# Half-tile input loads, a paced fold and single steps in the first block of an FFT-plus-ReGLU kernel

## The chip, the cores and the metric

The kernel runs on one core of a Trainium2 chip. The metric is the device time of one execution in microseconds (us). Engine names follow the profile: PE is the matmul engine, PEld its weight load, DVE the vector engine, ACT the scalar engine, POOL the GpSimd engine, SP the engine whose queue issues most DMAs.

Before the change the median was 692.59 us of three runs (692.4 to 693.47).

## The reference

```python
X = np.fft.fft(np.fft.fft(x, axis=1), axis=2).real     # x: 8 x 3008 x 256, float32
h = X.reshape(24064, 256)
out = (np.maximum(h @ w_gate, 0) * (h @ w_val)) @ w_out # 256 -> 1536 -> 256
```

The kernel never forms X in full. It uses the symmetry of the transform of a real signal: row s and row 3008 - s share most of their work. The second transform is folded into the weights at the start.

## The kernel before

Each of the 8 batches is three blocks of 12 steps, so there are 288 steps in 24 blocks. A step is one slice of 128 hidden columns: gate matmuls (`G`), value matmuls (`V`), and products of both, `h`. Two steps form a pair. A pair's direct products are made by DVE, its mirrored products by POOL (from batch 0's second block on). The output matmuls of a block run during the block after it.

While the steps of batch b run, the input of a later batch is prepared in three stages:

- The load: x of batch b+2 comes into `xl` (17 of 32 rows of each partition) and, in mirrored partition order by an indirect DMA on POOL, into `xh` (the other rows).
- The fold, on POOL: sums and differences of mirrored rows and columns, in pieces, into `eo`. It overwrites `xl` and reads `xh`; there is one buffer of each.
- Stage 1 for batch b+1: matmuls on `eo`, a copy to DRAM and back in another layout (the shuffle, `Td`), a small matmul (`rotate`), then stage 2, whose results `pq` and `nb` feed the steps.

```python
def load_x(b, q):
    xl = xp.tile([96, J, D], F32, tag="xl", name="xl")           # J = 17, D = 256
    xh = xp.tile([96, NB // 2, D], F32, tag="xh", name="xh")     # NB = 32
    for p0, n in ((0, 80), (80, 14)):
        q.dma_start(out=xl[p0:p0 + n], in_=...)
    nc.gpsimd.indirect_dma_start(out=xh[...], in_=..., in_offset=...ix[:, b:b + 1]...)
    xt[b] = (xl, xh, tp.tile([NA, J, D], BF16, tag="eo", name="eo"))

def fold(b, eng):                       # a generator: one piece at each yield
    for lo in range(1, J - 1, xc):      # xc is 3 for batches 1 and 2, then 2
        eng.tensor_tensor(...)                                    # L98
        yield eng.tensor_tensor(x1[:, :, 1:D], x1[:, :, 1:D], ...)  # L100
        for op, o in ((ALU.add, 1), (ALU.subtract, H + 1)):
            yield eng.tensor_tensor(e1[...], x1[:, :, 1:H], ...)  # L103
    # ... (the two end rows)

# first number: step of the load; second: step at which the fold begins; then stage 1,
# shuffle, rotate, stage 2 (all counted from the first step of the batch)
plan = {0: (18, 24, (18, 19, 20, 21, 22, 23, 24, 25), 26, 32, (33, 34, 35, 37, 39, 41)),
        1: (7, 13, (7, 8, 10, 11, 13, 14, 16, 17), 18, 25, (26, 28, 29, 31, 34, 35)),
        2: (7, 13, (4, 5, 7, 10, 11, 13, 16, 17), 18, 25, (26, 28, 29, 31, 34, 35))}

def between(t):                         # once a step
    for fn in extra.get(t, ()): fn()
    while folds and next(folds[0], folds) is folds:   # one fold piece a step
        folds.pop(0)

for p in range(n + NF // 2):            # the main loop, by pairs
    t = 2 * p
    ...
    # block 0 (split(t) is False): V gets direct and mirror parts one after the other, on DVE
    value(t, 0); value(t, 1); value(t + 1, 0); value(t + 1, 1)
    ...; direct_h(p)                    # both steps' direct products
    ...; value(t, 2); value(t + 1, 2)   # mirror parts, into the same accumulators
    # next iteration: mirror_value(p - 1), both steps' mirrored products
```

In block 0 POOL is still folding batch 1's x, so both products are made by DVE there, and the mirror part of `V` may only be added once DVE has used the direct part.

## Time and profile before

| what | value |
|---|---|
| median time | 692.59 us |
| profiled span | 691.2 us |
| a block without fold (batches 6 and 7) | 24.6 to 25.0 us |
| block 0 | 34.9 us |
| block 2 | 31.1 us |
| middle block of batches 2 to 5 | 27.8 to 29.4 us |

Block times are taken from the first gate activation of one block to that of the next. From the profile page of the kernel before: the span, the busy time of each engine with its share of the span, and the rows of PE, POOL and the granted clock (the share of its full clock that PE was given) over 40 equal slices in tenths (9 is 90% or more). The last line follows the chain of work that ended last back from the end, as shares of the span by engine.

```profile
span 691.2 us, 11747 instructions
...
PE 636.6 (92%) x4200; PEld 414.0 (60%) x4231; DVE 548.6 (79%) x630; ACT 432.7 (63%) x846; POOL 512.6 (74%) x412
...
PE   7776897998999989998999989998999999999995
...
POOL 9539458995999589975999579974999555555552
PEclk8799998999999999999999999999999999999998
...
PE 46%; POOL 24%; DMA 13%; DVE 7%; issue 5%; ACT 2%; SPq 1%; POOLq 0%; DVEq 0%; ACTq 0%
...
```

PE is near 9 in most slices and has dents at 7 and 8. From the 10th slice on, each dent stands beside or just behind a low POOL digit, after which POOL goes to 9: POOL waits and then has more than it can do at once. POOL and DMA make up 37% of the chain. The next excerpt, the list of waits, says for what (who waited for whom: us in total, times, longest).

```profile
...
POOL h L538 <- DVE E L546: 99.5, 57, 7.5
...
DVE E L525 <- POOL h L538: 42.3, 32, 4.1
...
POOL eo L98 <- DMA xl<-in_x_dram: 26.4, 4, 7.0
POOL eo L98 <- DMA xh<-in_x_dram,ix: 23.4, 3, 10.5
...
```

The first line costs nothing by itself: POOL is simply ahead. The last two lines are fold pieces that wait for their x to land, 49.8 us in seven waits. They matter because POOL works in order and mirrored products are queued behind the fold piece. The second line is DVE waiting for those products.

Busy time by stretch, for block 0, block 2, the middle and last block of batch 2, and a block without fold. The columns are the stretch and its length, then busy us (and instructions) of PE, PEld, DVE, ACT, POOL, the granted PE clock, the DMA share and GB/s.

```profile
...
38.51:73.41 34.90, 24.30 (x123) 9.66 (x123) 17.32 (x19) 15.64 (x30) 23.52 (x26) 0.95 0.49 94
99.32:130.40 31.08, 27.37 (x178) 17.46 (x176) 21.63 (x25) 17.68 (x35) 24.97 (x20) 0.89 0.42 118
236.68:264.96 28.28, 24.86 (x165) 16.43 (x166) 21.98 (x25) 16.68 (x34) 21.29 (x18) 1.00 0.51 131
264.96:290.35 25.39, 25.17 (x185) 16.79 (x183) 21.46 (x25) 18.21 (x37) 24.92 (x23) 1.00 0.20 52
550.48:575.52 25.04, 24.70 (x165) 16.42 (x166) 21.91 (x25) 16.79 (x35) 13.99 (x7) 1.00 0.39 104
...
```

In the last line PE is busy 24.70 of 25.04 us: this is the bound by PE. In the third, PE needs nearly the same, 24.86 us, but the block takes 28.28.

One of these waits on POOL's timeline (start, duration, what, and in brackets the idle time before it and what ended it), inside that block:

```profile
...
225.85 0.96 POOL L85 DMA_INDIRECT xh<-in_x_dram,ix  x1
...
235.78 2.30 POOL L538 TENSOR_TENSOR h<-gm,E 128x992 bf16<-128x992 f32 x1 [1.96 <-DVE E L546]
244.75 0.22 POOL L98 TENSOR_TENSOR eo<-xl,xh 94x4 bf16<-94x4 f32 x1 [6.68 <-DMA xl<-in_x_dram]
...
246.27 2.27 POOL L538 TENSOR_TENSOR h<-gm,E 128x992 bf16<-128x992 f32 x1
...
```

DVE in the same stretch:

```profile
...
243.83 1.22 DVE L531 TENSOR_TENSOR h<-gs,V 128x1024 bf16<-128x1024 f32 x1
248.57 1.41 DVE L525 SCALAR_TENSOR_TENSOR E<-nb,af,V 128x512 f32<-128x512 bf16 x2 [3.52 <-POOL h L538]
...
```

The indirect part of the load is issued at 225.85; the direct part, which the piece waits for here, follows on SP behind output stores at 227.0. The first fold piece can start only at 244.75, 6.68 us after POOL became free, and the mirrored product after it starts at 246.27. DVE stood idle for 3.52 us before 248.57, and the block is 3.2 us longer than one without a fold.

### The profile page before, as it was taken

Reading aid. Unit: us, or ns where it says so; the run is one execution under the profiler, and the core shown is the slowest. Engines: PE = TensorE matmul, PEld = TensorE weight load, DVE = VectorE, ACT = ScalarE, POOL = GpSimd, SP = SyncE. Lnnn points to the kernel's source line nnn. Section 1 sums busy time; section 2 is a strip of 40 time slices with the busy share of each in tenths; the row PEclk is TensorE's granted clock in tenths of the full one; section 3 lists DMA queues with packets and bytes.
Section 4 is the critical chain, followed back from the end, with each engine's and each line's share of the span. In section 5 each row is a group of like instructions: output and inputs, shape, how many; then the busy total and the mean of one; then the engine's idle time right before and its main releaser. Section 6 shows DMA issues by size and latency. Waiting matters only on the chain.

```text
span 691.2 us, 11747 instructions
## 1 busy us (share of the span) xinstructions
PE 636.6 (92%) x4200; PEld 414.0 (60%) x4231; DVE 548.6 (79%) x630; ACT 432.7 (63%) x846; POOL 512.6 (74%) x412
## 2 busy tenths in 40 slices
PE   7776897998999989998999989998999999999995
PEld 3322564665666656665666656666566666666664
DVE  9725885777888878887888878886888888888981
ACT  5444583766677756676676756766576766756660
POOL 9539458995999589975999579974999555555552
PEclk8799998999999999999999999999999999999998
DMA  9691095155511932246521942246421223312113
GB/s 247 211 219 20 15 208 160 48 132 122 151 47 39 219 102 77 76 114 141 147 51 39 210 109 80 61 116 154 122 70 46 55 81 79 82 30 49 41 32 90
DMA packets 33982, 70.71 MB, mean 102 GB/s; under 512 B 5802, under 2 KB 23186, under 8 KB 31922
## 3 DMA queue, kind: packets, MB, share of 16 engines
q1 hardware_dynamic: 31284, 57.92, 33.0%
q0 software_dynamic: 2336, 11.80, 8.0%
q8 instruction: 33, 0.54, 0.3%
q10 hardware_dynamic: 304, 0.25, 0.1%
q14 instruction: 25, 0.20, 0.1%
HBM read 39.77 MB, written 30.96 MB: 102 GB/s over the span
## 4 chain that ended last, share of the span: by engine, by line
PE 46%; POOL 24%; DMA 13%; DVE 7%; issue 5%; ACT 2%; SPq 1%; POOLq 0%; DVEq 0%; ACTq 0%
PE po L570 19%; PE V L518 12%; POOL h L538 10%; DMA xl<-in_x_dram 7%; POOL xl L100 5%; DMA xh<-in_x_dram,ix 5%; POOL eo L103 5%; DVE E L525 4%; PE G L504 4%; PE G L510 4%; PE G L503 4%; POOL eo L131 2%; PE psw L274 1%; DVE h L531 1%; SPq L621 1%
## 5 line engine op out<-in xcount | busy, mean ns | idle before, releaser
L538 POOL TENSOR_TENSOR h<-gm,E 128x992 bf16<-128x992 f32 (+1 forms) x138 | 319.6, 2316 | 99.5 <-DVE E L546 99.5
L570 PE MATMUL po<-wo,h 128*128 128x256 bf16 (+2 forms) x2304 | 343.5, 273 | 0.6
L570 PEld LDWEIGHTS <-h 128*128 128x128 bf16 (+2 forms) x2304 | 233.9, 103 | 122.0 <-issue 1.8
L525 DVE SCALAR_TENSOR_TENSOR E<-nb,af,V 128x496 f32<-128x496 bf16 (+1 forms) x276 | 191.0, 734 | 101.6 <-PE V L518 47.7
L512 ACT ACTIVATE gm<-G 128x496 f32<-128x496 f32 (+1 forms) x288 | 170.3, 591 | 154.3 <-PE G L510 131.3
L531 DVE TENSOR_TENSOR h<-gs,V 128x992 bf16<-128x992 f32 (+2 forms) x144 | 172.0, 1194 | 6.1 <-ACT gs L505 5.1
L505 ACT ACTIVATE gs<-G 128x497 f32<-128x497 f32 (+2 forms) x288 | 169.4, 588 | 1.4 <-PE G L504 1.4
L546 DVE SCALAR_TENSOR_TENSOR E<-E,V 128x992 f32<-128x992 f32 (+1 forms) x138 | 164.4, 1192 | 0.0
L504 PE MATMUL G<-pq,ws 128*128 128x497 bf16 (+2 forms) x288 | 108.5, 377 | 1.6 <-DVE pq L224 0.6
L518 PE MATMUL V<-pq,wc 128*128 128x497 bf16 (+2 forms) x288 | 109.0, 378 | 0.0
L510 PE MATMUL G<-pq,wm 128*128 128x496 bf16 (+1 forms) x288 | 108.9, 378 | 0.0
L518 PE MATMUL V<-pq,ws 128*128 128x496 bf16 (+2 forms) x276 | 83.9, 378 | 24.8 <-DVE E L525 22.0
L503 PE MATMUL G<-pq,wc 128*128 128x496 bf16 (+2 forms) x269 | 101.6, 378 | 0.0
L103 POOL TENSOR_TENSOR eo<-xl 94x254 bf16<-94x254 f32 (+2 forms) x100 | 73.9, 750 | 2.2
L100 POOL TENSOR_TENSOR xl<-xl,xh 94x510 f32<-94x510 f32 (+2 forms) x50 | 65.9, 1319 | 3.9
L583 ACT COPY os<-po 128x512 f32<-128x512 f32 x63 | 36.9, 586 | 34.8 <-PE po L570 32.9
L518 PEld LDWEIGHTS <-ws 128*128 128x128 bf16 x288 | 27.4, 97 | 42.1 <-issue 39.6
L504 PEld LDWEIGHTS <-ws 128*128 128x128 bf16 x288 | 28.4, 99 | 33.3 <-issue 1.3
L98 POOL TENSOR_TENSOR eo<-xl,xh 94x4 bf16<-94x4 f32 (+2 forms) x50 | 10.9, 219 | 49.8 <-DMA xl<-in_x_dram 26.4
L185 ACT CAST t<-ps 96x512 bf16<-96x512 f32 x63 | 36.7, 582 | 12.1 <-PE ps L173 7.3
L518 PEld LDWEIGHTS <-wc 128*128 128x128 bf16 x288 | 28.4, 99 | 21.4 <-issue 4.1
L503 PEld LDWEIGHTS <-wc 128*128 128x128 bf16 x288 | 28.4, 99 | 4.8 <-issue 0.3
(113 smaller groups left out, 330.2 us busy)
## 6 DMA issues: line engine op xcount, KB each, us to landing
out_dram<-os SPq DMA_DIRECT2D x126, 128.0 KB
xl<-in_x_dram SPq DMA_DIRECT2D x7, 1360.0 KB
out_dram<-os SPq DMA_DIRECT2D x86, 64.0 KB
Td<-t SPq DMA_DIRECT2D x7, 768.0 KB
t<-Td SPq DMA_DIRECT2D x7, 768.0 KB
nb<-Nd SPq DMA_DIRECT2D x24, 128.0 KB
out_dram<-os SPq DMA_DIRECT2D x39, 48.0 KB
xl<-in_x_dram SPq DMA_DIRECT2D x7, 238.0 KB
```

The lines of the kernel that those rows point to most:

```text
L103: yield eng.tensor_tensor(e1[:, :, o:o + H - 1], x1[:, :, 1:H], free(x1, D - 1, [D, n], [-1, H - 1]), op=op)
L503: nc.tensor.matmul(G[:, ds], lhsT=wc[0][:, fs], rhs=pq[:, 0, ds], start=True, stop=False)
L504: nc.tensor.matmul(G[:, ds], lhsT=ws[0][:, fs], rhs=pq[:, 1, ds], start=False, stop=True)
L505: nc.scalar.activation(pair(t, "gs")[:, t % 2, ds], G[:, ds], ACTF.Relu)
L510: nc.tensor.matmul(G[:, cols], lhsT=wm[0][:, f * 128:(f + 1) * 128], rhs=pqt[b, blk][:, 1, cols], start=False, stop=True, skip_group_check ...
L512: nc.scalar.activation(pair(t, "gm")[:, t % 2, cols], G[:, cols], ACTF.Relu)
L518: nc.tensor.matmul(pair(t, "V")[:, t % 2, cs], lhsT=w[:, f * 128:(f + 1) * 128], rhs=pqt[b, blk][:, min(k, 1), cs], start=(k == 0), stop=( ...
L525: nc.vector.scalar_tensor_tensor(pair(t, "E")[:, t % 2, cols], nbt[b, blk][:, cols], af[:, f:f + 1], pair(t, "V")[:, t % 2, cols], op0=ALU ...
L531: nc.vector.tensor_tensor(pair(t, "h")[:, :, 0, 0:ds.stop - ds.start], pair(t, "gs")[:, :, ds], pair(t, "V")[:, :, ds], op=ALU.mult)
L538: eng.tensor_tensor(free(pair(t, "h")[:], 512 + n - 1, [1024, 2], [-1, n]), pair(t, "gm")[:, :, cols], val[:, :, cols], op=ALU.mult)
L546: nc.vector.scalar_tensor_tensor(E[:, :, cols], E[:, :, cols], 2.0, V[:, :, cols], op0=ALU.mult, op1=ALU.subtract)
L570: nc.tensor.matmul(po[0:m, i, :], lhsT=pair(t - f + ff, "h")[:, ff % 2, sg, g * 128:g * 128 + m], rhs=wo[:, ff, :], start=(ff == 0), stop= ...
```

## The change

The tiles are split into halves (`xla`, `xha`, `xlb`, `xhb`). A half of the next batch's x is asked for as soon as the same half of the current one is folded. The fold is given out at a fixed pace of pieces a step instead of one a step from a set start. Block 0 is run by single steps, so that the products of one step overlap the mirror matmul of the step before.

```diff
+    def load_x(b, half, q):
+        xl, xh = xt.setdefault(b, {})[half] = (x_tile(True, half), x_tile(False, half))
+        ...                       # two DMAs on SP, one indirect DMA on POOL, for half the rows
     def fold(b, eng):
-        for lo in range(1, J - 1, xc):
+        for half, chunks in enumerate(((1, 3, 5, 7), (9, 11, 13))):
+            for lo in chunks:     # three pieces each, as before
+                ...
+            ...                   # the end row of this half, one piece
+            yield eo
+            if 1 < b < B - 1:
+                load_x(b + 1, half, nc.sync)
 ...
-        if b + 2 < B:
-            at(t0 + tl, load_x, b + 2, nc.sync)
-            at(t0 + tf, lambda b=b: folds.append(fold(b + 2, nc.gpsimd)))
+    for half in range(2):
+        at(14, load_x, 2, half, nc.sync)
+    folds = itertools.chain.from_iterable(fold(b, nc.gpsimd) for b in range(2, B))
+    def pace(t):
+        paced["due"] += 0 if t < 22 else 1 if t < 46 else 0.85 if t < 100 else 0.7
+        while paced["due"] >= 1:
+            paced["due"] -= 1
+            next(folds, None)
 ...
+    for t in range(NF + 1):                       # block 0
+        if t:
+            mirror_gate(t - 1)
+        if t < NF:
+            gate(t)
+        if t:
+            value(t - 1, 2)
+            mirror_h(t - 1, 1, nc.vector, pair(t - 1, "V"))
+        if t < NF:
+            value(t, 0); value(t, 1); direct_h(t, 1); between(t)
-    for p in range(n + NF // 2):
+    for p in range(NF // 2, n + NF // 2):         # the rest by pairs, as before
```

(Shortened. Stage 1 of batch 2 also starts three steps later, and a fold now has 23 pieces where batches 3 to 7 had 26.)

More of the change, by code (lines that the diff above doesn't have):

```diff
@@ L75, with x_tile @@
     xt = {}
-    XC = 3
-    def load_x(b, q):
-        xl = xp.tile([96, J, D], F32, tag="xl", name="xl")
-        xh = xp.tile([96, NB // 2, D], F32, tag="xh", name="xh")
-        for p0, n in ((0, 80), (80, 14)):
-            q.dma_start(out=xl[p0:p0 + n],
-                        in_=view(x, b * S * D + p0 * NB * D, [[NB * D, n], [1, J * D]]))
+    JH = NB // 4
+    def x_tile(low, half):
+        name = f"x{'hl'[low]}{'ab'[half]}"
+        return xp.tile([96, JH + (low and not half), D], F32, tag=name, name=name)
@@ L85, in load_x @@
+    def load_x(b, half, q):
+        xl, xh = xt.setdefault(b, {})[half] = (x_tile(True, half), x_tile(False, half))
+        n, j0 = (JH, JH + 1) if half else (JH + 1, 0)
+        for p0, np_ in ((0, 80), (80, 14)):
+            q.dma_start(out=xl[p0:p0 + np_],
+                        in_=view(x, b * S * D + (p0 * NB + j0) * D, [[NB * D, np_], [1, n * D]]))
         nc.gpsimd.indirect_dma_start(out=xh[:].rearrange("p j d -> p (j d)"), out_offset=None,
-                                     in_=view(x, 0, [[NB * D // 2, 2 * B * NA], [1, NB * D // 2]]),
@@ L87, in load_x @@
-                                     in_offset=bass.IndirectOffsetOnAxis(ap=ix[:, b:b + 1], axis=0))
-        xt[b] = (xl, xh, tp.tile([NA, J, D], BF16, tag="eo", name="eo"))
+                                     in_=view(x, 0, [[JH * D, 4 * B * NA], [1, JH * D]]),
+                                     in_offset=bass.IndirectOffsetOnAxis(ap=ix[:, half, b:b + 1], axis=0))
     def fold(b, eng):
-        xl, xh, eo = xt[b]
-        xc = XC if b < 3 else 2
-        for lo in range(1, J - 1, xc):
-            n = min(xc, J - 1 - lo)
-            x1, e1, m = xl[0:NA, lo:lo + n, :], eo[:, lo:lo + n, :], (NB // 2 - lo) * D
-            eng.tensor_tensor(free(e1, 0, [D, n], [H, 2]), free(x1, 0, [D, n], [H, 2]),
-                              free(xh[0:NA], m, [-D, n], [H, 2]), op=ALU.add)
-            yield eng.tensor_tensor(x1[:, :, 1:D], x1[:, :, 1:D], free(xh[0:NA], m + D - 1, [-D, n], [-1, D - 1]),
-                                    op=ALU.add)
-            for op, o in ((ALU.add, 1), (ALU.subtract, H + 1)):
-                yield eng.tensor_tensor(e1[:, :, o:o + H - 1], x1[:, :, 1:H], free(x1, D - 1, [D, n], [-1, H - 1]),
-                                        op=op)
@@ L105, in fold @@
-        ends = free(xl[0:NA], 0, [(J - 1) * D, 2], [H, 2])
-        eng.tensor_copy(free(eo[:], 0, [(J - 1) * D, 2], [H, 2]), ends)
-        for op, o in ((ALU.add, 1), (ALU.subtract, H + 1)):
-            yield eng.tensor_tensor(
-                free(eo[:], o, [(J - 1) * D, 2], [1, H - 1]), free(xl[0:NA], 1, [(J - 1) * D, 2], [1, H - 1]),
-                free(xl[0:NA], D - 1, [(J - 1) * D, 2], [-1, H - 1]), op=op)
+        eo = xt[b]["eo"] = tp.tile([NA, J, D], BF16, tag="eo", name="eo")
+        for half, chunks in enumerate(((1, 3, 5, 7), (9, 11, 13))):
+            xl, xh = xt[b][half]
+            for lo in chunks:
+                n, o = (3 if lo == 13 else 2), lo - half * (JH + 1)
+                x1, e1, m = xl[0:NA, o:o + n, :], eo[:, lo:lo + n, :], (NB // 2 - lo - (0 if half else JH)) * D
+                eng.tensor_tensor(free(e1, 0, [D, n], [H, 2]), free(x1, 0, [D, n], [H, 2]),
+                                  free(xh[0:NA], m, [-D, n], [H, 2]), op=ALU.add)
+                yield eng.tensor_tensor(x1[:, :, 1:D], x1[:, :, 1:D],
+                                        free(xh[0:NA], m + D - 1, [-D, n], [-1, D - 1]), op=ALU.add)
+                for op, o in ((ALU.add, 1), (ALU.subtract, H + 1)):
+                    yield eng.tensor_tensor(e1[:, :, o:o + H - 1], x1[:, :, 1:H],
+                                            free(x1, D - 1, [D, n], [-1, H - 1]), op=op)
+            src, j = xl[0:NA, JH - 1 if half else 0, :], J - 1 if half else 0
+            eng.tensor_copy(free(eo[:], j * D, [H, 2]), free(src, 0, [H, 2]))
+            for op, o in ((ALU.add, 1), (ALU.subtract, H + 1)):
+                eng.tensor_tensor(eo[:, j, o:o + H - 1], src[:, 1:H], free(src, D - 1, [-1, H - 1]), op=op)
+            yield eo
+            if 1 < b < B - 1:
+                load_x(b + 1, half, nc.sync)
@@ L113 @@
     FIRST = (0, 28, 4, 24, 8, 20, 12, 16)
     def load_first():
-        xl = xp.tile([96, J, D], F32, tag="xl", name="xl")
-        xh = xp.tile([96, NB // 2, D], F32, tag="xh", name="xh")
+        t = {0: x_tile(True, 0), 1: x_tile(True, 1), 2: x_tile(False, 1), 3: x_tile(False, 0)}
         for r in FIRST:
-            nc.sync.dma_start(out=(xl if r < 16 else xh)[:, r % 16:r % 16 + 4, :],
+            nc.sync.dma_start(out=t[r // JH][:, r % JH:r % JH + 4, :],
                               in_=view(x, r * D, [[NB * D, 96], [1, 4 * D]]))
-        xt[0] = [xl, xh] + [tp.tile([NA, J, D], BF16, tag="eo", name="eo") for i in range(2)]
+        t["e"] = [tp.tile([NA, J, D], BF16, tag="eo", name="eo") for i in range(2)]
@@ L123, in fold_first @@
+        xt[0] = t
     def fold_first(r, n, op, eng):
-        t, e = xt[0][r // 16][0:NA], xt[0][2 + r // 16]
+        t, e = xt[0][r // JH][0:NA], xt[0]["e"][r // 16]
         lo = r % 16
         def part(a, n, o, op, swap):
-            p0 = free(t, a * D + 1, [D, n], [1, H - 1])
-            p1 = free(t, a * D + D - 1, [D, n], [-1, H - 1])
+            p0 = free(t, (a % JH) * D + 1, [D, n], [1, H - 1])
+            p1 = free(t, (a % JH) * D + D - 1, [D, n], [-1, H - 1])
             eng.tensor_tensor(e[:, a:a + n, o:o + H - 1], p1 if swap else p0, p0 if swap else p1, op=op)
@@ L134, in fold_first @@
             part(lo, n, 1, ALU.add, False)
-            eng.tensor_copy(free(e[:], lo * D, [D, n], [H, 2]), free(t, lo * D, [D, n], [H, 2]))
+            eng.tensor_copy(free(e[:], lo * D, [D, n], [H, 2]), free(t, (lo % JH) * D, [D, n], [H, 2]))
         elif r == 16:
@@ L164, in stage1 @@
             t1t[b] = tp.tile([96, 16, D], BF16, tag="t1", bufs=1, name="t1")
-        t1, eo = t1t[b], xt[b][2]
-        eh = xt[b][3] if b == 0 else None
+        t1 = t1t[b]
+        eo, eh = xt[b]["e"] if b == 0 else (xt[b]["eo"], None)
         ps = early("ps1") if b == 0 else borrow("ps1")
@@ L229, in stage2 @@
             nc.sync.dma_start(out=nbt[b, blk][:], in_=view(row, 0, [[0, 128], [1, 512]]))
-    ix = const.tile([96, B], I32, tag="ix")
+    ix = const.tile([96, 2, B], I32, tag="ix")
     w1 = const.tile([NA, 16, 96], BF16, tag="w1")
@@ L440 @@
         dve.tensor_copy(rot[:], ro[:].rearrange("p u s j -> p (u s j)"))
-        pl.iota(ix[:], pattern=[[2 * NA, B]], base=2 * NA - 1, channel_multiplier=-2)
+        pl.iota(ix[:], pattern=[[-1, 2], [4 * NA, B]], base=4 * NA - 1, channel_multiplier=-4)
         pl.tensor_scalar(ix[:], ix[:], scalar1=0, scalar2=None, op0=ALU.max)
@@ L449 @@
         pl.tensor_copy(seen[:, 0:1], t4t[0][0:1, NKA - 1, 0:1])
-        load_x(1, nc.sync)
+        for half in range(2):
+            load_x(1, half, nc.sync)
         pl.dma_start(out=wo[:], in_=view(w_out, 0, [[D, 128], [128 * D, NF], [1, D]]))
@@ L526, in even, with direct_h, mirror_h @@
                                        pair(t, "V")[:, t % 2, cols], op0=ALU.mult, op1=ALU.add)
-    def direct_h(p):
-        t = 2 * p
-        ds = direct(t)
-        nc.vector.tensor_tensor(pair(t, "h")[:, :, 0, 0:ds.stop - ds.start], pair(t, "gs")[:, :, ds],
-                                pair(t, "V")[:, :, ds], op=ALU.mult)
-    def mirror_h(p, eng, val):
-        t = 2 * p
-        cols = mirrored(t)
-        n = cols.stop - cols.start
-        eng.tensor_tensor(free(pair(t, "h")[:], 512 + n - 1, [1024, 2], [-1, n]), pair(t, "gm")[:, :, cols],
-                          val[:, :, cols], op=ALU.mult)
+    def direct_h(t, n):
+        ds, k = direct(t), slice(t % 2, t % 2 + n)
+        nc.vector.tensor_tensor(pair(t, "h")[:, k, 0, 0:ds.stop - ds.start], pair(t, "gs")[:, k, ds],
+                                pair(t, "V")[:, k, ds], op=ALU.mult)
+    def mirror_h(t, n, eng, val):
+        cols, k = mirrored(t), slice(t % 2, t % 2 + n)
+        w = cols.stop - cols.start
+        eng.tensor_tensor(free(pair(t, "h")[:], 1024 * (t % 2) + 512 + w - 1, [1024, n], [-1, w]),
+                          pair(t, "gm")[:, k, cols], val[:, k, cols], op=ALU.mult)
     def mirror_value(p):
@@ L543, in mirror_value @@
         cols = mirrored(t)
-        if split(t):
-            E, V = pair(t, "E"), pair(t, "V")
-            nc.vector.scalar_tensor_tensor(E[:, :, cols], E[:, :, cols], 2.0, V[:, :, cols],
-                                           op0=ALU.mult, op1=ALU.subtract)
-            mirror_h(p, nc.gpsimd, E)
-        else:
-            mirror_h(p, nc.vector, pair(t, "V"))
+        E, V = pair(t, "E"), pair(t, "V")
+        nc.vector.scalar_tensor_tensor(E[:, :, cols], E[:, :, cols], 2.0, V[:, :, cols],
+                                       op0=ALU.mult, op1=ALU.subtract)
+        mirror_h(t, 2, nc.gpsimd, E)
     state = {}
@@ L636 @@
     at(9, nyquist)
-    plan = {0: (18, 24, (18, 19, 20, 21, 22, 23, 24, 25), 26, 32, (33, 34, 35, 37, 39, 41)),
-            1: (7, 13, (7, 8, 10, 11, 13, 14, 16, 17), 18, 25, (26, 28, 29, 31, 34, 35)),
-            2: (7, 13, (4, 5, 7, 10, 11, 13, 16, 17), 18, 25, (26, 28, 29, 31, 34, 35))}
-    for b in range(B):
+    plan = {0: ((18, 19, 20, 21, 22, 23, 24, 25), 26, 32, (33, 34, 35, 37, 39, 41)),
+            1: ((10, 11, 13, 14, 16, 17, 19, 20), 21, 28, (29, 31, 32, 34, 35, 37)),
+            2: ((4, 5, 7, 10, 11, 13, 16, 17), 18, 25, (26, 28, 29, 31, 34, 35))}
+    for b in range(B - 1):
         t0 = b * NBLK * NF
-        tl, tf, t1, tsh, tr, t2 = plan[min(b, 2)]
-        if b + 2 < B:
-            at(t0 + tl, load_x, b + 2, nc.sync)
-            at(t0 + tf, lambda b=b: folds.append(fold(b + 2, nc.gpsimd)))
-        if b + 1 < B:
-            for c, k in zip((1, 2, 3, 4, 5, 6, 7, 0), t1):
-                at(t0 + k, stage1, b + 1, c, "act")
-            at(t0 + tsh, shuffle_out, b + 1, 0, 8)
-            at(t0 + tsh, shuffle_in, b + 1, 0, NKA)
-            at(t0 + tr, rotate, b + 1)
-            for i, k in enumerate(t2):
-                at(t0 + k, stage2, b + 1, i // 2, i % 2, "act")
-    folds = []
+        t1, tsh, tr, t2 = plan[min(b, 2)]
+        for c, k in zip((1, 2, 3, 4, 5, 6, 7, 0), t1):
+            at(t0 + k, stage1, b + 1, c, "act")
+        at(t0 + tsh, shuffle_out, b + 1, 0, 8)
+        at(t0 + tsh, shuffle_in, b + 1, 0, NKA)
+        at(t0 + tr, rotate, b + 1)
+        for i, k in enumerate(t2):
+            at(t0 + k, stage2, b + 1, i // 2, i % 2, "act")
+    for half in range(2):
+        at(14, load_x, 2, half, nc.sync)
+    folds = itertools.chain.from_iterable(fold(b, nc.gpsimd) for b in range(2, B))
+    paced = {"due": 0.0}
+    def pace(t):
[3 more added lines that the diff above has]
+            next(folds, None)
     n = len(steps) // 2
-    def fill(t, half):
-        if t >= NF:
-            out_piece(t - NF, half)
     def between(t):
@@ L666, in between @@
             fn()
-        while folds and next(folds[0], folds) is folds:
-            folds.pop(0)
-    for p in range(n + NF // 2):
+        pace(t)
+    for t in range(NF + 1):
[7 more added lines that the diff above has]
+        if t < NF:
+            value(t, 0)
+            value(t, 1)
+            direct_h(t, 1)
+            between(t)
+    for p in range(NF // 2, n + NF // 2):
         t = 2 * p
         live = p < n
-        if 0 < p <= n:
+        if NF // 2 < p <= n:
             mirror_gate(t - 1)
@@ L677 @@
             value(t, 0)
-            if not split(t):
-                value(t, 1)
-        fill(t, 0)
+        out_piece(t - NF, 0)
         between(t)
@@ L683 @@
             value(t + 1, 0)
-            if not split(t):
-                value(t + 1, 1)
-        if 0 < p <= n:
-            (direct_h if split(t - 1) else mirror_value)(p - 1)
+        if NF // 2 < p <= n:
+            direct_h(t - 2, 2)
         if live:
-            if split(t):
-                even(t)
-                even(t + 1)
-        fill(t, 1)
+            even(t)
+            even(t + 1)
+        out_piece(t - NF, 1)
         if live:
@@ L695 @@
             gate(t + 1)
-            if not split(t):
-                direct_h(p)
-        fill(t + 1, 0)
+        out_piece(t + 1 - NF, 0)
         between(t + 1)
-        if 0 < p <= n and split(t - 1):
+        if NF // 2 < p <= n:
             mirror_value(p - 1)
         if live:
-            for k in range(2):
-                value(t + k, 1 if split(t) else 2)
-        fill(t + 1, 1)
+            value(t, 1)
+            value(t + 1, 1)
+        out_piece(t + 1 - NF, 1)
 _INS = ['x', 'moe_w_gate', 'moe_w_val', 'moe_w_out']
```

## The prediction

> **What bounds the kernel now.** The page's busy shares are PE 92%, DVE 79%, POOL 74%, ACT 63%. Most of the span is 24 blocks of 12 steps. I cut it at the first gate activation (`gs`) of each block and read busy times per stretch. Blocks without folds (batch 6 and 7) take 24.6 to 25.0 us, with PE busy 24.3 to 24.9: PE-bound. Others are longer:
> - Block 0: 34.9 us with PE busy 24.3.
> - Block 2: 31.1 us, clock 0.89.
> - The middle block of batches 1 to 5: 27.8 to 29.4 us.
> - The remaining fold blocks: 25.4 us, POOL busy 24.95, so POOL-bound.
>
> The waits explain this. POOL runs a batch's fold and the mirror products (`h`, L538, 2.3 us a pair) in one order. In batches 1 to 5 the first fold piece waits for the newly loaded x (L98 waits for DMA: 49.8 us in all, 6.7 to 10.5 us each) with `h` behind it. DVE then waits for POOL (E L525: 42.3 us, 32 times), and PE behind DVE. Near 239 to 246 us POOL waits 6.7 us and DVE 3.5 us.
>
> **What the change does.**
> 1. Loads. Each half of x is reloaded as soon as it is folded, 10 to 13 fold pieces (over 24 us) before its next use. A whole load takes 13 to 18.5 us from issue to landing, so the DMA waits should vanish from batch 3 on; fold 2 is loaded at step 14, used from step 22 (about 17 us), and should barely wait.
> 2. Pacing. Now 26 pieces follow one another at one per step: 2 x 1.01 + 2.3 = 4.33 us of POOL a pair, against 4.13 for PE. A fold becomes 23 pieces, some longer: 6 x 3.04 + 4.15 + 2 x 1.15 = 24.7 us, plus a second indirect issue (0.96 us each), about 27 us. At 0.7 a step POOL needs about 3.97 us a pair: under PE. At 0.85 (steps 46 to 99) about 4.31, slightly over; at 1.0 (steps 22 to 45) about 4.6, over, partly hidden by the three E buffers.
> 3. Block 0 by single steps. DVE and PE now alternate idle there (PE waits 0.9 to 2.5 us for DVE each pair; a pair takes 4.85 to 6.3 us). With singles, step t's product overlaps step t-1's mirror matmul. From the traced durations (0.6 us a single product, 0.37 matmul, 0.69 casts, 1.08 weight fold) I estimate 1.75 to 3.2 us a step, 29.7 us in all.
>
> **Estimate by blocks** (now, after): prologue 38.5, 38.5; block 0 34.9, 29.7; 1: 25.9, 25.7; 2: 31.1, 26.5; 3: 27.2, 27.0; 4 to 8: 132.7, 129; 9 to 16: 210.7, 200.4; 17 to 22: 148.9, 148.9; last 41.5, 41.5. Span about 667, time about **669 us**, range 660 to 681. Chances: faster by over 2% 0.85, within 2% 0.13, slower 0.02.
>
> The Trainium skill ("TensorE: Matmul & The Clock Gate", Part 1) says an idle PE is dropped to half clock after about 3.4 us. This trace agrees: half-clock stretches of 3.4 to 6.8 us at 44, 112 and 484 us follow PE stalls; I expect the last two gone.
>
> **Right or wrong will show in:** L98's DMA waits under 5 us beyond the first; E waiting for POOL under 15 us; L85 14 times; POOL under 96% busy from step 100; block 0 near 30 us; no middle-block bump.
>
> **What would break it:** stage 1 reaching PE before the paced fold is done; half loads colliding with the shuffle through DRAM (10 us, 4 us of slack); the load's wait for POOL holding SP's stores; block 0 still gated by ACT behind DVE casts.

## The result, and the profile after

The changed kernel takes 667.08 us (median of 4 runs, 666.22 to 669.18) against 692.5 us for the kernel before (4 runs). The ratio is 0.9636, 95% interval 0.9611 to 0.9661. Ratios here and below are the mean time of one kernel's fast runs over that of the other's of the same rounds, so not quite the ratio of the medians that are quoted. The profiled run is the slowest of the four (669.18 us, span 667.4), which matters below.

The page of the changed kernel, the same parts:

```profile
span 667.4 us, 11836 instructions
...
PE 631.6 (95%) x4200; PEld 411.5 (62%) x4231; DVE 549.7 (82%) x642; ACT 433.2 (65%) x846; POOL 521.5 (78%) x436
...
PE   6867999999999999999999998999999999999995
...
POOL 9559679999999999999988996988555555555552
PEclk9699999999999999999999998999999999999998
...
PE 78%; DVE 9%; POOL 5%; DMA 3%; issue 2%; ACT 2%; SPq 0%; DVEq 0%; POOLq 0%; ACTq 0%
...
```

PE is at 9 nearly everywhere now, with one dent left in the 25th slice, where the clock row has one too, and POOL and DMA are down to 8% of the chain. The list of waits:

```profile
...
POOL h L547 <- DVE E L554: 107.7, 70, 4.1
...
PE V L527 <- DVE h L547: 7.7, 6, 1.7
...
POOL eo L105 <- DMA xha<-in_x_dram,ix: 6.2, 1, 6.2
...
PE psr L213 <- DMA t<-Td: 2.6, 1, 2.6
...
DVE E L534 <- POOL h L547: 2.1, 2, 1.4
...
```

One wait for x is left, 6.2 us, in batch 1's own fold at the start. DVE's wait for POOL's products (the last line) fell from 42.3 to 2.1 us; with the waits put down to fold pieces it is 8.2 us in 12 times, before it was 45.7 us in 40. PE still waits for a product of DVE in block 0, now the mirrored one (7.7 us in 6 times); before, it was the direct one (`PE V L518 <- DVE h L531`, 10.5 us in 6). A wait for the shuffle (`t<-Td`) is new.

The stretches that answer to those shown before: block 0, block 2, the middle and last block of batch 2, and last the slow last block of batch 4.

```profile
...
38.39:71.45 33.06, 23.88 (x122) 8.88 (x122) 19.65 (x32) 15.52 (x29) 25.65 (x35) 1.00 0.55 104
97.00:121.83 24.83, 24.74 (x178) 16.44 (x176) 21.46 (x25) 17.56 (x35) 24.36 (x24) 1.00 0.43 112
223.19:248.22 25.03, 24.69 (x165) 16.43 (x166) 21.89 (x25) 16.77 (x34) 24.55 (x24) 1.00 0.58 159
248.22:273.51 25.29, 24.92 (x185) 16.62 (x183) 21.52 (x25) 18.29 (x37) 24.73 (x22) 1.00 0.46 126
398.40:427.60 29.20, 26.58 (x185) 17.36 (x183) 21.61 (x25) 18.41 (x36) 22.53 (x19) 0.94 0.35 88
...
```

POOL on either side of a half load, in the middle block of batch 2:

```profile
...
230.90 0.85 POOL L115 TENSOR_TENSOR eo<-xla 94x127 bf16<-94x127 f32 x2
231.72 2.35 POOL L547 TENSOR_TENSOR h<-gm,E 128x1024 bf16<-128x1024 f32 x1
234.22 0.95 POOL L92 DMA_INDIRECT xha<-in_x_dram,ix  x1 [0.15 <-issue]
235.20 0.24 POOL L105 TENSOR_TENSOR eo<-xlb,xhb 94x4 bf16<-94x4 f32 x1
...
```

As soon as the end piece of the first half is done, the same half of the next batch is asked for (234.22). The next piece, from the other half, follows with no wait: it was asked for 33 us earlier, at 202.2 us.

Where the time came from, by the profiled spans. The column "predicted" is the prediction's own sum.

| part | before | predicted | after |
|---|---|---|---|
| up to the first gate activation | 38.5 | 38.5 | 38.4 |
| block 0 | 34.9 | 29.7 | 33.1 |
| blocks 1 to 3 | 84.2 | 79.2 | 75.9 |
| blocks 4 to 8 | 132.7 | 129.0 | 126.2 |
| blocks 9 to 16 | 210.4 | 200.4 | 203.9 |
| blocks 17 to 22 | 148.9 | 148.9 | 148.9 |
| last block and the tail | 41.5 | 41.5 | 41.1 |
| span | 691.2 | 667.2 | 667.4 |

(For blocks 9 to 16 before, the prediction has 210.7; the trace gives 210.4.) The sum is right to 0.2 us, but it is right by errors of 3 us that cancel. Three questions are therefore open. Is it the early load, the halves or the pacing that brings the gain? Why did block 0 give 1.8 us where 5.2 were expected? And where do the 3.5 us beyond the forecast in blocks 9 to 16 come from?

### The profile page after: what moved, and what is told of

Read it like the earlier page. It is cut to its first block, busy times and chain, and to the rows that moved or that the text cites. A ratio compares the mean times of both kernels' runs of the same rounds, so it can differ in the third digit from the quotient of the medians.

```text
span 667.4 us, 11836 instructions
## 1 busy us (share of the span) xinstructions
PE 631.6 (95%) x4200; PEld 411.5 (62%) x4231; DVE 549.7 (82%) x642; ACT 433.2 (65%) x846; POOL 521.5 (78%) x436
## 4 chain that ended last, share of the span: by engine, by line
PE 78%; DVE 9%; POOL 5%; DMA 3%; issue 2%; ACT 2%; SPq 0%; DVEq 0%; POOLq 0%; ACTq 0%
PE po L576 32%; PE V L527 19%; PE G L513 8%; PE G L519 7%; PE G L512 7%; DVE E L534 6%; DMA t<-Td 2%; PE ps L183 2%; POOL eo L139 2%; PE ps L225 1%; POOL h L547 1%; PE psw L282 1%; DVE h L540 1%; DVE h L547 1%; DMA nb<-Nd 1%
## 5 line engine op out<-in xcount | busy, mean ns | idle before, releaser
L534 DVE SCALAR_TENSOR_TENSOR E<-nb,af,V 128x496 f32<-128x496 bf16 (+1 forms) x276 | 190.9, 733 | 79.2 <-PE V L527 61.5
L540 DVE TENSOR_TENSOR h<-gs,V 128x1024 bf16<-128x1024 f32 (+3 forms) x150 | 172.7, 1151 | 8.6 <-PE V L527 7.5
L527 PEld LDWEIGHTS <-wc 128*128 128x128 bf16 x288 | 28.2, 98 | 20.9 <-issue 3.2
L110 POOL TENSOR_TENSOR eo<-xla 94x254 bf16<-94x254 f32 x56 | 40.0, 724 | 1.0
L107 POOL TENSOR_TENSOR xla<-xla,xha 94x510 f32<-94x510 f32 x28 | 35.4, 1264 | 2.2
L110 POOL TENSOR_TENSOR eo<-xlb 94x254 bf16<-94x254 f32 (+1 forms) x42 | 33.6, 809 | 0.7
L519 PEld LDWEIGHTS <-wm 128*128 128x128 bf16 x288 | 28.2, 98 | 6.9 <-issue 4.1
```

The source lines that it names most:

```text
L110: yield eng.tensor_tensor(e1[:, :, o:o + H - 1], x1[:, :, 1:H], free(x1, D - 1, [D, n], [-1, H - 1]), op=op)
L519: nc.tensor.matmul(G[:, cols], lhsT=wm[0][:, f * 128:(f + 1) * 128], rhs=pqt[b, blk][:, 1, cols], start=False, stop=True, skip_group_check ...
L527: nc.tensor.matmul(pair(t, "V")[:, t % 2, cs], lhsT=w[:, f * 128:(f + 1) * 128], rhs=pqt[b, blk][:, min(k, 1), cs], start=(k == 0), stop=( ...
L534: nc.vector.scalar_tensor_tensor(pair(t, "E")[:, t % 2, cols], nbt[b, blk][:, cols], af[:, f:f + 1], pair(t, "V")[:, t % 2, cols], op0=ALU ...
L540: nc.vector.tensor_tensor(pair(t, "h")[:, k, 0, 0:ds.stop - ds.start], pair(t, "gs")[:, k, ds], pair(t, "V")[:, k, ds], op=ALU.mult)
```

## The experiments

Eleven kernels ran, all with correct results, five rounds each. Experiments of one call share their runs of the kernel before; 1 and 3 to 5 are the first call, 6 to 9 the second, 10 and 11 the third, 12 the fourth. No run isolates one part of the change, the start of stage 1 of batch 2 three steps later.

### 1. The first block alone

The kernel before, with the single-step loop of the change for block 0. Nothing else differs.

```diff
 # kernel before
-    for p in range(n + NF // 2): ...
+    for t in range(NF + 1): ...          # as in the change
+    for p in range(NF // 2, n + NF // 2): ...
```

> The kernel before, with only its first block run by single steps; loads and folds untouched. Theory A (the parts add up, and the first block is worth what the trace of the changed kernel shows there): block 0 goes from 34.9 to about 33.1 us, the rest stays (middle blocks 28 us, POOL still waits about 50 us for DMA), so 690.5 to 691.5 us. Rival B (the first block is also what lets POOL start its later folds in time, so it is worth more than its own 1.8 us): 685 us or less. The prediction on record had 5.2 us for this part: 687.3 us.

Measured: 691.52 us against 692.79, ratio 0.9992 (0.9970 to 1.0014), so by the clock alone not to be told from no change. In the trace block 0 takes 33.07 us, as in the changed kernel (33.06). POOL still waits 48.4 us for x, and the later blocks together are as long as before (617.2 us against 617.8). This is Theory A, and Rival B is out. Block 0 is worth at most 1.8 us and helps nothing else, so nearly all of the 24 us comes from the loads and the fold.

Even the 1.8 us are not all due to the single steps. In the profiled run of the kernel before, PE ran at half clock for 3.4 us of block 0 (from 43.98 us), and in that of the changed kernel it did not. Experiment 6 has the old block 0 and no such stretch there, and its block 0 takes 33.31 us. At full clock the single steps of the change are thus worth about 0.2 us.

### 3. Early halves, fold in bursts

The changed kernel, but the pieces are given out one a step from the steps at which the kernel before began its folds.

```diff
 # changed kernel
-        paced["due"] += 0 if t < 22 else 1 if t < 46 else 0.85 if t < 100 else 0.7
-        while paced["due"] >= 1: ...
+        k = t // 36
+        opened = 24 * (k + (t % 36 >= (13 if k else 24)))
+        if paced["due"] < opened:
+            paced["due"] += 1
+            if paced["due"] % 24: next(folds, None)
```

> The changed kernel, with half loads as early as before but the fold pieces one per step from the same steps as in the kernel before (step 24, then step 13 of each batch), not paced. Theory A (the early half loads are the larger part of the gain, pacing the smaller): DMA waits of POOL stay under 10 us, the middle blocks stay near 25.5 us instead of 28, and fold blocks run at the POOL-bound 25.4 us; 668 to 672 us. Rival B (pacing is what matters: POOL bursts make DVE and PE wait whatever the loads do): middle blocks back at 27 us or more, 677 us or more.

Measured: 666.27 us, ratio 0.9634 (0.9614 to 0.9654), level with the changed kernel's 0.9636. The middle blocks stay at 25.0 to 25.5 us. Theory A (668 to 672 us) expected the fold blocks at 25.4 us, from the third blocks of the kernel before; from batch 3 on the first and third blocks are at 24.96 to 25.00. Bursts have a price only early, in blocks 5 and 6 (26.00 and 25.55 us against 24.74 and 24.82), and they spare block 14 the shortfall that the next experiment is about (24.96 against 29.20). Over the whole run pacing buys nothing that can be measured here. The fairer comparison is with run 4 below, which keeps the pacing and has no such shortfall: its median is 0.6 us lower, and the intervals overlap. The result also means that the prediction's "POOL-bound" reading of those 25.4 us was wrong: the same rate of pieces does not slow PE unless POOL starts late.

### 4. One load moved off a shuffle

In the profiled run of the changed kernel the last block of batch 4 is 4.2 us longer than it should be. PE there, around the `rotate` matmul:

```profile
...
402.89 0.18 PE L213 MATMUL psr<-t,rot 128*128 128x12 bf16 x1 [2.56 <-DMA t<-Td]
...
403.97 0.62 PE L519 MATMUL G<-pq,wm 128*128 128x496 bf16 x1
...
```

PE waited 2.56 us for the shuffle's read, and then ran at half clock (a matmul of 0.37 us takes 0.62). The DMA packets show why. The read of the shuffle is 1,536 packets of 512 bytes on SP's queue. Normally the last one ends 4.0 to 4.8 us after the read is issued. In this one it ends after 8.24 us, and 96 packets of 8,192 bytes of the indirect half load, on POOL's queue, start inside. That part of the load had been issued 0.3 us before the read. (The direct part, on SP's queue, was issued 0.5 us after the read; 36 of its packets start inside, near the end.) The Trainium skill ("DMA: Bandwidth & Descriptors", Queues, rings and completion order) says that each DMA engine takes turns between the queues it has work for, packet by packet, and the trace agrees with that picture: between 3 and 5 us after the issue, 63 packets of the read and 60 of the indirect load started, about one for one, where an undisturbed read (the one at 318.87 us) starts over 200 in each half microsecond. The experiment moves this load, both parts of it.

```diff
 # changed kernel
-            if 1 < b < B - 1:
+            if 1 < b < B - 1 and (b, half) != (6, 1):
                 load_x(b + 1, half, nc.sync)
+    at(171, load_x, 7, 1, nc.sync)
```

> The changed kernel, with one load moved: the second half of batch 7's x is asked for at step 171, after the rotation of batch 5, instead of at step 165, where its packets run beside the shuffle read. Theory A (that load delays the shuffle read, PE stalls 2.6 us and then loses its clock): the 2.6 us wait of the rotation for the shuffle and the half-clock stretch near 403 us are gone, block 14 falls from 29.2 to about 25.1 us, the profiled span to about 663 us, the median to 663 to 666 us. Rival B (the late shuffle comes from the stores and the shuffle's own traffic): block 14 stays above 28 us and the median within 1 us of 667.

Measured: the read takes 4.51 us, `rotate` does not wait, the clock is whole, and the block takes 24.96 us instead of 29.20. The profiled span is 664.8, not 663, since this run reached its first gate 1.5 us later. The median is 665.71 us, ratio 0.9607 (0.9588 to 0.9625). The cause of the long block is shown. What it costs in a usual run is less than in the profiled one: the medians differ by 1.4 us and the intervals overlap. How the collision falls in runs without a profile was not recorded, but one other profile hints at it: in experiment 5, where this load was not moved, the read again took 7.8 us and PE waited 1.79 us, but no half clock followed, and block 14 took 26.77 us. The collision can thus come without the half clock; how often it does is not shown.

### 5. A V tile for each step of block 0

In the changed kernel PE waits for DVE's mirrored product in block 0 six times, always before the first `V` matmul of the second step of a pair. PE:

```profile
...
51.31 0.37 PE L527 MATMUL V<-pq,wm 128*128 128x496 bf16 x1
53.43 0.37 PE L527 MATMUL V<-pq,wc 128*128 128x496 bf16 x1 [1.75 <-DVE h L547]
...
```

DVE at the same time:

```profile
...
52.70 0.67 DVE L547 TENSOR_TENSOR h<-gm,V 128x496 bf16<-128x496 f32 x1 [1.23 <-ACT gm L521]
54.11 0.67 DVE L540 TENSOR_TENSOR h<-gs,V 128x496 bf16<-128x496 f32 x1 [0.74 <-PE V L527]
...
```

The product of 52.70 reads the accumulator of the first step; the matmul of 53.43 writes that of the second. They lie in different halves of one tile. Each half is 512 float32 wide, 2 KiB a partition, which is the size of one bank as the Trainium skill gives it ("PSUM — Partial Sum Buffer", Terms), so the two should not meet. Still, the compiled matmul carries a wait for DVE. Then the direct product (54.11) waits for the matmul in turn: products and matmuls alternate, which the single steps were meant to end. The experiment gives each step of block 0 its own tile, and the two buffers of the pool alternate by step.

```diff
 # changed kernel
-        e = pairs.setdefault(t // 2, {})
+        e = pairs.setdefault(("V", t) if name == "V" and not split(t) else t // 2, {})
```

> The changed kernel, with a V tile of its own for each single step of block 0 (the pool's two buffers alternate by step, not by pair). Theory A (the second step of a pair waits for the mirror product of the first only because both lie in one tile): the waits of PE for that product in block 0, 7.7 us in 6 times, fall below 1.5 us, and block 0 falls from 33.1 to 28 to 31 us; 662 to 665.5 us. Rival B (block 0 is held by ACT behind the DVE casts and by the weight folds on PE): the waits only change their name, block 0 stays above 32 us, 666 us or more.

Measured: 660.35 us, ratio 0.9534 (0.9516 to 0.9552). Block 0 takes 27.02 us, better than Theory A's 28 to 31; PE's waits for the mirrored product are gone. PE at a second step of a pair:

```profile
...
48.96 0.37 PE L527 MATMUL V<-pq,wm 128*128 128x496 bf16 x1
49.17 0.37 PE L527 MATMUL V<-pq,wc 128*128 128x496 bf16 x1
...
```

The matmul follows the one before it by 0.21 us with no wait. So the wait was a matter of two steps sharing a tile, not of the banks. That the program's tracking of dependencies puts it in for the whole tile is the likely reason; only the effect of separate tiles was shown.

### 6. Whole loads, asked for earlier

Are halves needed at all? The kernel before asks for x at step 7, though the buffers come free some steps sooner. Here only that number is changed.

```diff
 # kernel before
-    plan = {0: (18, 24, ...   1: (7, 13, ...   2: (7, 13, ...
+    plan = {0: (14, 24, ...   1: (6, 13, ...   2: (3, 13, ...
```

> The kernel before, with one number changed per batch: the whole x is asked for at step 14 (was 18) of batch 0, step 6 (was 7) of batch 1 and step 3 (was 7) of every later batch, which is as soon as the fold that reads the buffers has been issued. The fold starts at the same step. Theory A (the loss was the wait of POOL for x, and any load that lands before the fold starts removes it; halves are only one way to that): the DMA waits of POOL fall from 49.8 to about 20 us (batch 1's own and the part of batch 3 remain), the middle blocks of batches 2 to 5 fall from 28 to 25 to 25.5 us, 674 to 680 us. Rival B (a whole load cannot be had early enough, or it collides with stores and shuffles, so halves are needed): middle blocks stay over 27 us, 686 us or more.

Measured: 672.12 us against 692.46, ratio 0.9700 (0.9680 to 0.9721): 20.3 us of the change's 25.4, from three numbers. Waits:

```profile
...
POOL eo L98 <- DMA xh<-in_x_dram,ix: 17.7, 2, 10.4
...
DVE E L525 <- POOL h L538: 9.7, 6, 4.0
...
```

Two waits for x are left: batch 1's own (10.4 us) and batch 3's (7.4 us). The middle blocks of batches 1 and 2:

```profile
...
150.26:180.40 30.14, 26.76 (x167) 17.45 (x168) 21.91 (x25) 17.36 (x36) 22.38 (x20) 0.94 0.48 130
230.12:255.16 25.04, 24.70 (x165) 16.43 (x166) 21.99 (x25) 16.78 (x35) 23.75 (x22) 1.00 0.41 110
...
```

Batch 1's (the first line), with batch 3's late x, takes 30.14 us. Batch 2's takes 25.04, where the kernel before had 28.28, and those of batches 3 to 5 are 25.04 too. Theory A holds, with a gain larger than it said.

### 9. Halves and pacing, but late loads

The changed kernel, except that each half of batches 3 to 7 is asked for two steps before its fold begins.

```diff
 # changed kernel
-            if 1 < b < B - 1:
-                load_x(b + 1, half, nc.sync)
+    at(43, load_x, 3, 0, nc.sync)
+    at(59, load_x, 3, 1, nc.sync)
+    ...                                  # eight more, each 2 steps before its fold
```

> The changed kernel, paced fold and halves kept, but each half load of batches 3 to 7 is asked for only 2 steps (about 4 us) before its fold's first piece. A half load takes 8 to 11 us from issue to landing. Theory A (a wait of POOL for x costs PE whatever the pacing, since the mirror products queue behind it): ten more waits of 3 to 6 us on POOL, 35 to 55 us in all, each costing 1 to 3 us, 680 to 695 us. Rival B (the paced POOL has slack enough to hide such waits, so it was pacing that cured the loss): 672 us or less in spite of the waits.

Measured: 703.49 us, ratio 1.0143 (1.0109 to 1.0177): 1.4% slower than the kernel before, clear of the noise. The waits:

```profile
...
DVE E L532 <- POOL h L545: 32.8, 7, 11.2
...
POOL eo L105 <- DMA xhb<-in_x_dram,ix: 13.9, 5, 6.2
POOL eo L105 <- DMA xla<-in_x_dram: 11.8, 1, 11.8
...
POOL eo L105 <- DMA xha<-in_x_dram,ix: 8.4, 2, 5.0
...
```

DVE waits again (32.8 us), though the fold is paced and POOL has slack. Six blocks are 3.3 to 8.6 us longer than in the changed kernel, 35 us together. (The half loads of the changed kernel took 6.6 to 11.1 us from batch 3 on, not 8 to 11.) Theory A holds in kind but was too low: the longest wait, 11.8 us, came where a late load met a shuffle, whose read then took 9.4 us, and its block took 37.8 us. So it is the moment at which x lands that decides, and neither halves nor pacing replace that.

### 7 and 8. Both remedies, and the order of two copies

Run 7 joins the edits of 4 and 5.

> The changed kernel with both remedies, a V tile per step in block 0 and batch 7's second half asked for after the shuffle. Theory A (they are independent): block 0 27.0 us, block 14 25.0 us, no rotation waits over 0.3 us for a shuffle read, median 658 to 659.5 us. Rival B (the second loss moves to another batch's shuffle): another block gets 1.5 us or more longer and the median stays at 660 us or more.

Measured: 659.06 us, ratio 0.9521 (0.9503 to 0.9538); block 0 27.02 us, block 14 24.96 us, no late rotation. The two are independent, as Theory A has it.

Run 8 also swaps two lines. When folded weights leave the accumulator, DVE makes a plain copy `ws` and ACT a scaled one `wm` of the same data. In the changed kernel ACT waits for DVE:

```profile
...
51.51 0.69 ACT L290 ACTIVATE wm<-psw,s 128x512 bf16<-128x512 f32 x1 [1.52 <-DVE ws L289]
...
```

The Trainium skill ("PSUM — Partial Sum Buffer", Terms) says that no two of PE, ACT and DVE may access one bank in the same partition at once, so one of the copies has to be first. This trace agrees in that the copies never overlap (in block 0 `wm` starts 0.03 to 0.04 us after `ws` ends). With `wm` second, ACT stands still 1.5 us, and both gate activations of the next step are queued behind.

```diff
 # run 7
-            plain(ws[i][:, sl_], ps[:])
             nc.scalar.activation(wm[i][:, sl_], ps[:], ACTF.Copy, scale=s2[:])
+            plain(ws[i][:, sl_], ps[:])
```

> As the run before, and in the folding of the weights ACT makes its scaled copy before DVE makes the plain one; both read the same accumulator, so one must wait for the other. Theory A (in steps 0, 4 and 6 of block 0 the chain cast on DVE, scaled copy on ACT, then both gate activations sets the step): these steps fall from 3.0 to 3.5 us to 2.4 to 2.8 us, block 0 from 27.0 to 25 to 26 us, median about 657.5 us. Rival B (DVE's products then wait behind its later cast instead): no change, within 0.5 us of the run before.

Measured: 657.50 us, ratio 0.9498 (0.9480 to 0.9515). In run 8 these copies wait for the matmul alone. The same copy, now at 48.37 us, waits 0.80 us, and so does the next one:

```profile
...
53.11 0.69 ACT L289 ACTIVATE wm<-psw,s 128x512 bf16<-128x512 f32 x1 [0.80 <-PE psw L282]
...
```

Steps 0, 4 and 6 fall from 3.13, 3.16 and 3.49 us to 2.41, 2.44 and 2.44; block 0 takes 25.49 us. Theory A holds.

### 10. A gentler pace at the start

Run 8, with 0.85 pieces a step from step 22 instead of 1.0 up to step 46.

```diff
 # run 8
-        paced["due"] += 0 if t < 22 else 1 if t < 46 else 0.85 if t < 100 else 0.7
+        paced["due"] += 0 if t < 22 else 0.85 if t < 100 else 0.7
```

> As the run e8, with 0.85 pieces a step from step 22 on in place of 1.0 up to step 46. Theory A (blocks 3 and 4 are 0.7 to 1.2 us over the blocks of later batches because POOL is over its share at 1.0 and 0.85 a step, as the prediction on record had it): blocks 2 to 4 lose 0.5 to 1.5 us together, 656.3 to 657 us. Rival B (0.85 is as bad, or what lengthens them is stage 1's own timing): within 0.5 us of 657.5.

Measured: 657.26 us, ratio 0.9501 (0.9480 to 0.9522), no change by the clock. The trace says why. Blocks 2 to 4 lost 1.4 us together (76.6 to 75.3), as Theory A expected. But the other pace moved a load onto batch 3's shuffle: 96 indirect packets inside the read, which took 7.2 us; `rotate` waited 1.5 us and block 8 took 26.52 us instead of 25.28. The load had been issued 1.0 us before the read, and the first packet of the read started only 3.66 us after its issue (1.0 to 1.1 us in undisturbed reads), behind nearly all of the load's. A gain was given back at another place.

### 11. Whole loads, no pacing, fold begun later

The kernel before with block 0 as in run 8, and with two kinds of numbers changed in the plan.

```diff
 # kernel before, with block 0 as in run 8
-    plan = {0: (18, 24, ...   1: (7, 13, ...   2: (7, 13, ...
+    plan = {0: (14, 24, ...   1: (7, 16, ...   2: (7, 16, ...
```

> The kernel before with whole loads and no pacing, but batch 0's load at step 14 and every later batch's fold begun at step 16 instead of 13 (9 steps after its load instead of 6), and block 0 as in the run e8. Theory A (all that the loads and the fold had to give was that x lands before its fold begins; halves and pacing are not needed for it): POOL waits for x only in batch 1's fold (10 to 11 us), middle blocks 25.0 to 25.5 us, 656 to 660 us, level with e8. Rival B (halves and pacing give something of their own beyond the wait): 664 us or more.

Measured: 660.79 us, ratio 0.9551 (0.9530 to 0.9572). This lies between the theories, nearer to A. From block 4 on it is level with run 8: middle blocks of 25.04 to 25.39 us and third blocks of 24.96 us, although these folds are the old ones, 26 pieces at one a step. The difference to run 8, 3.3 us by the medians, is in blocks 2 and 3: 26.42 and 27.45 us against 24.84 and 25.76. There the fold of batch 2 begins at step 24 rather than 22, in larger pieces, and stage 1 of batch 2 has its old, earlier place. The later begin is not the cause: experiment 3 begins at step 24 too, with the smaller pieces and the later stage 1, and its blocks 2 and 3 take 24.84 and 25.02 us. With the larger pieces POOL's products start 4.86 us apart (95.90 to 120.21 us, five pairs), with the smaller ones of experiment 3 4.15 us (100.24 to 121.01), and DVE waits 7.8 us for them in these blocks of run 11. That speaks for the size of the pieces; but no run separates it from the place of stage 1. So one of these two, or both, are worth about 3 us at the start, and nothing later.

### 12. A pace that misses the shuffles

The changed kernel with the edits of 5 and 8, no load moved by hand, and a pace picked by counting steps so that no half load is asked for within three steps of a shuffle.

```diff
 # changed kernel, with the edits of 5 and 8
-        paced["due"] += 0 if t < 22 else 1 if t < 46 else 0.85 if t < 100 else 0.7
+        paced["due"] += 0 if t < 22 else 0.85 if t < 60 else 0.66
```

> The changed kernel with a V tile per step in block 0, the scaled weight copy first, and a pace of 0.85 a piece up to step 60, then 0.66, chosen so that by count of steps no half load is asked for within 3 steps of a shuffle; no load is moved by hand. In the run e10 the earlier pace had put a load beside batch 3's shuffle (the rotation waited 1.5 us, block 8 took 26.5 us). Theory A (the rotation stalls follow the loads' place against the shuffles): no rotation wait over 0.3 us after the first, block 8 25.0 to 25.3 us, block 14 25.0 us, 655 to 656.5 us. Rival B (with faster kernels some shuffle is late anyway): a rotation wait of over 1 us somewhere, 657 us or more.

Measured: 655.46 us (655.17 to 655.74, 5 runs), ratio 0.9477 (0.9461 to 0.9494), the fastest of all. After the first rotation none waits, every shuffle read takes 4.2 to 4.5 us, no block from 1 to 22 takes over 25.84 us, and the clock is never halved between the first block and the tail. Theory A holds.

## Why the prediction was right or wrong

**The time was right**: 669 us forecast, 667.08 measured, inside the range, and faster by 3.6%. That it came so close is luck: the parts were off by about 3 us each, in both directions.

**The main mechanism was right.** POOL's waits for x, with the mirrored products queued behind them, were the loss. POOL's waits for x went from 49.8 to 6.2 us, the middle blocks from 27.8 to 29.4 us down to 25.0 to 25.4 (26.3 in batch 1). Experiments 6 and 9 show it from both sides: earlier loads alone bring 20.3 us, late loads with everything else kept cost more than the whole gain.

**"POOL-bound" third blocks and the cost of the pace were wrong.** The prediction read the 25.4 us of the remaining fold blocks as POOL's limit, and expected 4.6 us of POOL a pair at one piece a step, over PE's 4.13, and so 26.5 and 27.0 us for blocks 2 and 3. They took 24.83 and 25.47. In the trace POOL needed 4.26 us a pair there, from the starts of four products (96.41 to 109.20 us, three pairs): two pieces cost 2.0 us, not about 2.15 (24.7 us over 23 pieces), and an indirect issue falls into few pairs. That the rest of the excess was taken up by the three `E` buffers, as the prediction had it in part, is likely and not shown. Experiments 3 and 11 show that from batch 3 on a fold at one piece a step leaves the third blocks at 24.96 us when it starts on time; the 25.4 of before is POOL catching up after its late start. For pacing as a part of its own, no gain could be told. The expected difference between 1.0 and 0.7 a step was mis-sized; what there is of it lies at the start (experiment 10: 1.4 us in blocks 2 to 4).

**Block 0 was wrong**: 29.7 us forecast, 33.06 measured. The failed step is "with singles, step t's product overlaps step t-1's mirror matmul". At every second step it does not, since the two steps of a pair share a tile (7.7 us of PE waits). With separate tiles, experiment 5, it takes 27.02 us. The 34.9 us that the prediction set out from also held a half-clock stretch: at full clock the old block 0 takes 33.31 us (experiment 6). The last of the things listed as what would break it, ACT behind the DVE casts, was real as well: 1.5 us of block 0 (experiment 8).

**The collision was named but not sized.** "Half loads colliding with the shuffle through DRAM" stood among the risks, with 4 us of slack. It happened once in the profiled run: 2.56 us of wait and a half-clock stretch of 3.4 us, 4.2 us in block 14. That error and those of the two points above cancel in the sum.

**The checks set in advance.** Waits for x beyond the first under 5 us: none is left. E waiting for POOL under 15 us: 2.1 for the products, 8.2 with all of POOL. The indirect load 14 times: 7 and 7. POOL under 96% busy from step 100: 194.2 of 220.8 us, 88%, up to step 204. No middle-block bump: so, but for 26.3 us in batch 1. Block 0 near 30 us: no. The two later half-clock stretches, at 112 and 484 us, are gone as expected, but a new one came at 404. Two readings in the prediction were loose. It gave the seven waits for x as 6.7 to 10.5 us each, and they were 5.6 to 10.5. And it held that its trace agrees with half clock after about 3.4 us of idling: PE's stalls at the stretches of 44, 112 and 484 us were 2.53, 3.68 and 2.90 us, and one of 2.93 us at 169 us had none.

## What to carry to other kernels

When an in-order engine both prepares the next input and feeds the bottleneck, look first at whether the input lands before its first use is queued: here moving that one issue by one to four steps brought 80% of what a rewrite with halves and pacing did. An early load is also a load beside something else, so place it by what else is in the DMA queues at that step, and look again whenever the pace changes. Before believing that a finer schedule overlaps, check that the finer pieces do not share a tile: a wait that ends with a product of the neighbouring step tells of that.

## What the Trainium skill lacked or had wrong

- "DMA: Bandwidth & Descriptors", Queues, rings and completion order: it gives the taking of turns by packets, but not what it costs a read in small packets. Here a read of 1,536 packets of 512 bytes took 4.0 to 4.8 us undisturbed and 7.8 to 8.2 us with 96 packets of 8,192 bytes of another queue inside it (9.4 us with 74 of them and 74 of 9,216 bytes on its own queue). Where the other load was 1.0 us ahead, the read began 2.6 us late instead (experiment 10, 7.2 us).
- "DMA: Bandwidth & Descriptors", Anatomy of one DMA: its fit of 2.0 us plus bytes over 436 GB/s gives, as an estimate, 3.8 us for an indirect half load of 96 x 8,192 bytes. From issue to landing it took 6.6 to 11.1 us from batch 3 on, with the direct load of the same half and the stores in the queues at the same time. No run here had a half load alone, so the fit itself is not tested.
- "TensorE: Matmul & The Clock Gate", Part 1: it gives half clock after an idle window of about 3.4 us. Here half-clock stretches came with single PE waits of 2.56 us (at 403 us), 2.53 us (at 44 us in the kernel before) and 2.15 us (experiment 1, at 403 us), while waits of 2.53 us (before, at 62 us) and 2.93 us (before, at 169 us) were followed by none. The length of a single wait did not decide it in these runs.
- No page has it: two banks in one tile were treated as one by the waits of the compiled program, 7.7 us of PE waits in block 0, gone with a tile for each.
